# Conditional expert-weight loads in 1 MB pieces, and the weight conversion's DMAs issued at another point of the slot

## The chip, the cores and the metric

One Trainium2 chip, one of its cores. The metric is device time in microseconds (us) from launch to end, all in one program. A profiled execution also has a span, from its first to its last instruction.

## The reference

Three stages, each feeding the next, all in float32 results:

```python
# 1: attention, 8 x 8 heads, 576 tokens, head size 64, 32 memory slots
a = softmax(phi over tokens);  k_m = a^T k;  v_m = a^T v
x = softmax(q k_m^T / 8) v_m                    # -> [4608, 512]
# 2: top-1 mixture of 8 experts, 512 -> 1024 -> 512
e = argmax of the normalised x . expert_emb / tau;  g = its probability
x = g * (relu(x @ w1[e]) @ w2[e])
# 3: bilinear layer, 512 -> 1024 -> 1024 -> 512
out = ((x @ v1) * (x @ v2)) @ w3 @ w_out
```

The weights of stage 3 arrive as 64-bit floats. They have to be turned into 32-bit ones by integer operations on the chip.

## The kernel before

Matrix products are done to float32 accuracy by splitting each operand into a high and a low part and adding three products (`mm3`, lines 113 to 116, so a matmul shows there under line 114, 115 or 116).

Stage 2, the mixture, is the stage that is changed. The tokens are sorted by expert into slots of 128; a slot has one expert. `Moe.run` (line 1558) goes over 36 slots j; a few further slots are handled by `single` (line 1538) if they are used. Iteration j does the first product of slot j (`mm1`, output `hp`, 24 matmuls of 512 columns) and the second product of slot j-2 (`mm2`, output `py`, 24 matmuls). Between the two the hidden block must be transposed, and this goes through DRAM:

- `flip(j)` (line 1432): VectorE transposes 32 x 32 blocks of slot j+3's gathered tokens (line 1439) and of `hp` (line 1445) into the tile `T`, of which there is one, and SP (SyncE) issues the write of `T` to a DRAM scratch `scr` (line 1450, 768 KB). I call this the T write of iteration j.
- `unflip` (line 1453): four loads from `scr` into the tile `U`, of which there are two (line 1458, 4 x 192 KB). They are issued by SP when the T write has landed. I call these the U loads.
- `splith(j-1)` (line 1474), in iteration j: ScalarE makes the high part `hTh` (line 1481) from U of slot j-1, VectorE the low part `hTl` (line 1483). `splitx` makes the operands of a later `mm1` from the same U.

ScalarE, VectorE and SP each work through their instructions in program order. So VectorE does, in iteration j: `flip(j)`, a branch for an expert change in w1 (`split1`, line 1372), half of `splith(j-1)`, a branch for w2 (`split2`, line 1382), the other half, `splitx`, then `out2` of slot j-2 (line 1524), and the weight conversion described below.

Expert weights: w1 and w2 of an expert are 2 MB each, held raw in four tiles of 512 KB each (`r1`, `r2`, lines 1292 and 1293), and split into high and low parts (`share`, line 1355) when the next slot has another expert. Every iteration issues, on SP, eight conditional loads of 512 KB (`load1`, `load2`, lines 1335 to 1353): pieces 2 and 3 of w1 and of w2 behind the T write, pieces 0 and 1 of both behind the U loads. The condition is a register, read by SP once per slot (`regs`, lines 1330 and 1331). Where the expert does not change, a conditional load moves nothing, but SP still goes through its instructions. In this data four changes of expert lie in the loop.

The weight conversion for stage 3 is spread over the slots by `Moe2.early(s)` (line 1934), with s = j - 2, called at the end of iteration j (the argument `late`, line 1612; the argument `early`, line 1589, is empty). It has two DMA parts on SP: `load_raw` (line 1648, 512 KB of 64-bit weights into a tile `st`, shown in the trace as `st<-in_moe_w_dram`, 16 times, s from 0 to 22) and `keep` (line 1671, 512 KB of converted weights to DRAM, `wq<-w` at line 1672, 8 times, s from 4 to 25). Its compute part is `conv` (line 1656: one instruction on ScalarE, four on VectorE), two steps after the load. At steps s from 25 on, `early` also issues loads and transposes that prepare stage 3.

So SP's order in iteration j is: T write; w1 pieces 2, 3; w2 pieces 2, 3; four U loads; the register reads; w1 pieces 0, 1; w2 pieces 0, 1; a `keep` or a `load_raw` or both, in most iterations up to j = 27; then the T write of j+1.

Stage 3 follows (`Moe2.run`, line 1967): first 8 plain column groups, then four groups by a seven-product scheme for 2 x 2 blocks (`pair`, line 1860), whose matmuls are at line 1811.

Of the kernel before, what the change touches and what calls it, by code (L numbers as in the profile page):

```python
# [8 lines left out]
F32 = mybir.dt.float32  # L9
# [7 lines left out]
P = 128  # L17
B, H, S, D, M = 8, 8, 576, 64, 32
N = B * S
DM = H * D  # L20
E, F = 8, 1024
# [97 lines left out]
class Fillers:  # L119
    def __init__(self):  # L120
        self.q = []
# [4 lines left out]
    def run(self, n):  # L126
        while n > 0 and self.q:
            self.q.pop(0)()
            n -= 1
# [1158 lines left out]
class Moe:  # L1288
    def __init__(self, c, pool, w1, w2, xs, ys):
        self.c, self.pool = c, pool  # L1290
        self.w1, self.w2, self.xs, self.ys = w1, w2, xs, ys
        self.r1 = [pool.tile([P, F], F32, name=f"w1r{k}") for k in range(4)]
        self.r2 = [pool.tile([P, 2, DM], F32, name=f"w2r{k}") for k in range(4)]
        self.s1 = [
            (pool.tile([P, F], F32R, name=f"w1h{k}"), pool.tile([P, F], F32R, name=f"w1l{k}")) for k in range(4)
        ]
        self.xg, self.xT, self.h, self.hT = {}, {}, {}, {}
        self.sreg, self.py, self.u = {}, {}, {}
# [34 lines left out]
        return self.sreg[j]  # L1333

    def load1(self, j, ks=range(4)):
        e, f = self.regs(j)
        kw = {} if f is None else {"cond": f}
        for k in ks:
            self.c.nc.sync.dma_start(
                out=self.r1[k],  # L1340
                in_=self.w1[bass.ds(e, 1), k * P:(k + 1) * P, :].rearrange("a p f -> p (a f)"),
                **kw,
            )

    def load2(self, j, ks=range(4)):
        e, f = self.regs(j)
        kw = {} if f is None else {"cond": f}
        for k in ks:
            self.c.nc.sync.dma_start(
                out=self.r2[k],  # L1350
                in_=self.w2[bass.ds(e, 1), 2 * k * P:(2 * k + 2) * P, :].rearrange("a (u p) f -> p (a u) f", u=2),
                **kw,
            )

# [183 lines left out]
    def single(self, j):  # L1538
        c, nc = self.c, self.c.nc
        r = nc.values_load(c.nused[0:1, 0:1], min_val=0, max_val=NSLOT)  # L1540
        with c.tc.If(r > j):
# [13 lines left out]
            if j + 1 < NSLOT:  # L1555
                self.single(j + 1)

    def run(self, early, late):
        g = self.gates

        def groups(j, f, d):
            for a, b in ((j - j % GS, j - j % GS + GS), (NT, NT + 1)):
                if a == j - d or (a == NT and j == NT - 2 + d):
                    f(a, b)

        for j in range(NT):
            self.mm1(j)
            if j == 0:
                self.load1(0)
            if j < 2:  # L1570
                self.split1(j + 1)
            if j == 1:
                self.split2_first(2, 4)
            self.flip(j)
            if j < 2:
                self.load1(j + 1)
            else:
                if j > 2:
                    self.load1(j, (2, 3))
                self.load2(j - 2, (2, 3))  # L1580
                self.split1(j + 1)
            if j == 0:
                self.tx(2)
            if j + 4 <= NT:
                self.gather(j + 4)
            self.unflip()
            if j > 1:
                self.load1(j + 1, (0, 1))
            if j in early:
                early[j]()  # L1590
            if j == 1:
                self.load2(0, (0, 1))
            if j == 0:
                self.split2_first(0, 2)
            if j > 1:
                self.mm2(j - 2)
            if j > 0:
                self.splith(j - 1, (0,))
            if j > 1:
                self.split2(j - 1)  # L1600
                self.load2(j - 1, (0, 1))
            if j > 0:
                self.splith(j - 1, (1,))
            self.splitx(j + 2)
            if j == NEAR - 2:
                self.nexts()
            groups(j, g.norm, 0)
            groups(j, g.shift, 1)
            if j > 1:
                self.out2(j - 2)  # L1610
            groups(j, g.finish, 1)
            if j in late:
                late[j]()
        self.mm2(NT - 2)
        self.load2(NT - 2, (2, 3))
        self.splith(NT - 1, (0,))
        self.split2(NT - 1)
        self.load2(NT - 1)
        self.splith(NT - 1, (1,))
        self.out2(NT - 2)  # L1620
        self.mm2(NT - 1)
        self.out2(NT - 1)
        self.single(NT)


class Moe2:
# [304 lines left out]
            nc.scalar.copy(h, w[:, i])  # L1931
            nc.gpsimd.tensor_tensor(c.wpl[:, 2 * x + i, :], w[:, i], h.bitcast(F32), op=ALU.subtract)

    def early(self, s, pool):
        if s == 0:
            self.wpool = pool()
            self.mark = self.c.keep.tile([1, 1], F32, name="mark")
            self.wpt = {}
        for n in range(16):
            if s == self.at(n):  # L1940
                self.load_raw(n)
            if s == self.at(n) + 3 and n % 2:
                self.keep(n // 2)
        for n in range(16):
            if s == self.at(n) + 2:
                self.conv(n)
        if s in (25, 28):
            self.load_y(0, (s - 25) // 3)
        if s in (27, 29):
            self.flip_out(0, (s - 27) // 2)  # L1950
        if s in (28, 30):
            self.flip_in(0, (s - 28) // 2)
        if s in (29, 31):
            self.prep_plain((s - 29) // 2)
        if s in (27, 28):
            self.wload(s - 27)
        if s == 30:
            self.wsplit(0)
            self.wload(2)
        if s in (32, 33):  # L1960
            self.load_wp(s - 32)
# [95 lines left out]
@with_exitstack  # L2057
def kernel(
    ctx: ExitStack,
    tc: tile.TileContext,  # L2060
    q: bass.AP,
    k: bass.AP,
    v: bass.AP,
    phi: bass.AP,
    emb: bass.AP,
    tau: bass.AP,
    w1: bass.AP,
    w2: bass.AP,
    m2w1: bass.AP,
    m2w2: bass.AP,  # L2070
    m2w3: bass.AP,
    m2wout: bass.AP,
    const: bass.AP,
    out: bass.AP,
):
    nc = tc.nc
    c = Ctx()
    c.nc, c.tc = nc, tc
    c.keep = ctx.enter_context(tc.tile_pool(name="keep", bufs=1))
    dram = ctx.enter_context(tc.tile_pool(name="dram", bufs=1, space=bass.MemoryType.DRAM))  # L2080
    xs = dram.tile([N, XW], F32, name="xs")
    ys = dram.tile([N, YW], F32, name="ys")
    ctx.enter_context(tc.manual_schedule())
    c.wp = dram.tile([F, DM], F32, name="wp")
    c.wq = [dram.tile([P, 1024], F32, name=f"wq{i}") for i in range(8)]
    c.scr2 = [dram.tile([P, 4, 256], F32, name=f"scry{i}") for i in range(4)]
    c.scr = [dram.tile([P, 4, SH], F32, name=f"scr{i}") for i in range(4)]

    def pool(name, **kw):
        return tc.tile_pool(name=name, bufs=1, reuse_waits="tile", **kw)  # L2090

    def pspool(name):
        return pool(name, space=bass.MemoryType.PSUM)

    c.psw = ctx.enter_context(pspool("psw"))
    psa = ExitStack()
    c.ps = psa.enter_context(pspool("psa"))
    rst = ExitStack()
    c.rt = rst.enter_context(pool("rt", side="right"))
    with pool("attn", side="left") as p, pool("wprod", side="left") as pw:  # L2100
        setup_const(c, p, const, emb, tau)
        at = Attn(c, p, pw, q, k, v, phi, xs, m2w3, m2wout)
        at.run()
    mst = ExitStack()
    moe = Moe(c, mst.enter_context(pool("moe", side="left")), w1, w2, xs, ys)
    moe.second(mst.enter_context(pool("moeb", side="left")))
    rp = rst.enter_context(pool("rout", side="right"))

    moe.load1(-1)
    moe.load2(-1)  # L2110
    for j in range(3):
        moe.gather(j)
    moe.gates = Gates(c, mst.enter_context(pool("gates", side="left")))
    psa.close()
    psb = ExitStack()
    c.ps = psb.enter_context(pspool("psm"))
    moe.split1(0)
    moe.tx(0)
    at.wp.tail(moe.pool2)
    moe.tx(1)  # L2120
    moe.gates.rows(rp)
    rst.close()
    moe.gather(3)
    est = ExitStack()
    moe2 = Moe2(c, m2w1, m2w2, ys, out)
    mk = lambda: est.enter_context(pool("m2a", side="right"))

    steps = range(NT - 34, NT)
    moe.run({}, {j: (lambda s=j - steps[0]: moe2.early(s, mk)) for j in steps})
    mst.close()  # L2130
    with pool("moe2", side="left") as p:
        moe2.run(p)
    est.close()
    psb.close()
# [58 lines left out]
```

## Time and profile before

| what | value |
|---|---|
| median of 3 runs | 1320.77 us (1313.59 to 1321.11) |
| the profiled execution's own time | 1324.6 us |
| its span | 1322.8 us |
| TensorE busy, share of the span | 1208.6 us, 91% |
| VectorE, ScalarE, GpSimd busy | 877.7, 496.2, 569.8 us |
| mean granted TensorE clock | 0.968 |
| bytes moved by DMA | 228.66 MB |

How to read it: the profiled execution is one run, 3.8 us above the median of the unprofiled ones. The 1.8 us between its own time and its span lie outside the program's instructions. A busy TensorE is not TensorE at its peak, because matmuls overlap: a matmul row lasts about 0.4 us while a new one starts every 0.23 us. The mixture's loop runs from about 270 to 730 us of the span.

### The profile page before, as it was taken

The page shows a single profiled execution, that of the slowest core. Times are in us where ns is not written, and L with a number is a line of the kernel's source. Part 1 is how long each engine was busy: PE and PEld are TensorE (multiplying, and loading weights), DVE is VectorE, ACT ScalarE, POOL GpSimd, SP SyncE. Part 2 cuts the span into 40 slices and gives each one's busy share as a digit, 9 for nine tenths or more (in the row PEclk, how much of TensorE's full clock was granted, in tenths as well). Part 3 has the DMA queues.
Part 4 walks back from the last instruction along what each step waited for, and adds up shares of the span by engine and source line. Part 5 has one row for each costly group of instructions (what it writes and reads, how often), then busy time and mean ns, then how long its engine had stood idle before and what let it go on. Part 6 is the DMA issues. An engine that isn't in the chain of part 4 may idle for free. (4 is left out here: it accounts for less than half of the span.)

```text
span 1322.8 us, 19897 instructions
## 1 busy us (share of the span) xinstructions
PE 1208.6 (91%) x6124; PEld 948.9 (72%) x6124; DVE 877.7 (66%) x1706; ACT 496.2 (38%) x897; POOL 569.8 (43%) x705
## 2 busy tenths in 40 slices
PE   7788789899988998998899899999999999999996
PEld 6555566677767776776667677887878787788885
DVE  5898999876566667547666266728763874687262
ACT  4655455342233233123333154425433533435330
POOL 2685766622132232222232038715761674376222
PEclk9879889999999999999999899999999999999998
DMA  9999996567998778887876164415241532332001
GB/s 238 248 241 258 235 259 204 190 204 222 283 267 250 221 219 272 239 227 230 274 224 176 58 216 133 128 61 146 64 143 48 144 96 96 101 90 96 32 17 64
DMA packets 115215, 228.66 MB, mean 173 GB/s; under 512 B 11720, under 2 KB 73160, under 8 KB 115088
## 3 DMA queue, kind: packets, MB, share of 16 engines
q1 hardware_dynamic: 105824, 197.75, 52.5%
q0 software_dynamic: 8832, 28.92, 6.8%
q8 instruction: 50, 0.82, 0.3%
q14 instruction: 77, 0.63, 0.2%
q10 hardware_dynamic: 432, 0.55, 0.1%
HBM read 292.39 MB, written 72.40 MB: 276 GB/s over the span
## 5 line engine op out<-in xcount | busy, mean ns | idle before, releaser
L1483 DVE SCALAR_TENSOR_TENSOR hTl<-U,hTh 128x128 fp32r<-128x128 f32 x288 | 81.3, 344 | 117.7 <-ACT hTh L1481 89.9
L115 PE MATMUL hp<-w1l,xTh 128*128 128x512 f32 x296 | 122.1, 412 | 21.5 <-DVEq L1379 16.8
L114 PE MATMUL hp<-w1h,xTh 128*128 128x512 f32 x296 | 120.6, 408 | 14.1 <-ACT w1h L1359 10.9
L114 PE MATMUL py<-w2h,hTh 128*128 128x512 f32 x296 | 119.5, 404 | 10.9 <-ACTq L1385 10.9
L1529 POOL DMA_INDIRECT ys<-y,sidx x37 | 37.4, 1011 | 206.7 <-DVE y L1528 145.0
L1481 ACT ACTIVATE hTh<-U 128x512 fp32r<-128x512 f32 x72 | 45.3, 631 | 210.2 <-DMA U<-scr 108.1
L115 PE MATMUL py<-w2l,hTh 128*128 128x512 f32 x296 | 118.7, 401 | 1.3 <-DVE w2l L1360 0.8
L116 PE MATMUL py<-w2h,hTl 128*128 128x512 f32 x296 | 118.4, 400 | 1.4 <-DVE hTl L1483 1.4
L116 PE MATMUL hp<-w1h,xTl 128*128 128x512 f32 x296 | 119.2, 403 | 0.0
L1713 DVE TENSOR_TENSOR wgl<-sum,wgh 128x1024 fp32r<-128x1024 f32 x32 | 45.7, 1429 | 103.3 <-ACT wgh L1709 103.1
L116 PE MATMUL po<-wph,abl 128*128 128x512 f32 x288 | 112.8, 392 | 1.0 <-DVE abl L1858 0.7
L114 PE MATMUL po<-wph,abh 128*128 128x512 f32 x288 | 112.2, 390 | 0.0
L115 PE MATMUL po<-wpl,abh 128*128 128x512 f32 x288 | 112.1, 389 | 0.0
L1811 PE MATMUL pst<-xsh,wgh 128*128 128x512 f32 x256 | 101.2, 395 | 1.9 <-ACT pc L1879 1.5
L1713 POOL TENSOR_TENSOR wgl<-w,wgh 128x512 fp32r<-128x512 f32 x32 | 43.4, 1355 | 134.8 <-ACT wgh L1709 129.3
L1811 PE MATMUL pst<-xsl,wgh 128*128 128x512 f32 x256 | 100.3, 392 | 0.9 <-DVE xsl L1801 0.9
L1811 PE MATMUL pst<-xsh,wgl 128*128 128x512 f32 x256 | 100.0, 391 | 0.0
L115 PEld LDWEIGHTS hp<-w1l,xTh 128*128 128x128 f32 x296 | 57.5, 194 | 42.2 <-DVEq L1379 22.5
L114 PEld LDWEIGHTS hp<-w1h,xTh 128*128 128x128 f32 x296 | 57.3, 194 | 31.0 <-ACT w1h L1359 13.0
L114 PEld LDWEIGHTS py<-w2h,hTh 128*128 128x128 f32 x296 | 56.4, 191 | 27.8 <-ACTq L1385 13.5
L1857 ACT CAST abh<-pa 128x512 fp32r<-128x512 f32 x32 | 19.9, 622 | 148.5 <-DVE pa L1890 148.5
L115 PEld LDWEIGHTS py<-w2l,hTh 128*128 128x128 f32 x296 | 56.5, 191 | 16.1 <-DVEq L1385 1.7
(300 smaller groups left out, 3094.8 us busy)
## 6 DMA issues: line engine op xcount, KB each, us to landing
w2r<-in_moe_w_dram SPq DMA_DIRECT2D x152, 512.0 KB
w1r<-in_moe_w_dram SPq DMA_DIRECT2D x150, 512.0 KB
scr<-T SPq DMA_DIRECT2D x34, 768.0 KB
U<-scr SPq DMA_DIRECT2D x136, 192.0 KB
w<-wq SPq DMA_DIRECT2D x40, 512.0 KB
yin<-ys SPq DMA_DIRECT2D x36, 256.5 KB
qs<-in_q_dram SPq DMA_DIRECT2D x16, 576.0 KB
kv<-in_k_dram SPq DMA_DIRECT2D x32, 288.0 KB
```

The costliest lines, as they stand in the source:

```text
L114: nc.tensor.matmul(out, a[0], b[0], start=first, stop=False)
L115: nc.tensor.matmul(out, a[0], b[1], start=False, stop=False)
L116: nc.tensor.matmul(out, a[1], b[0], start=False, stop=last)
L1481: nc.scalar.activation(h4, u, ACTF.Relu)
L1483: nc.vector.scalar_tensor_tensor(l4[:, k], u[:, k], 0.0, h4[:, k].bitcast(F32), op0=ALU.max, op1=ALU.subtract)
L1529: nc.gpsimd.indirect_dma_start(out=self.ys, out_offset=bass.IndirectOffsetOnAxis(ap=c.sidx[:, j:j + 1], axis=0), in_=y, in_offset=None, bo ...
L1713: eng.tensor_tensor(l[:, s], src, h[:, s].bitcast(F32), op=ALU.subtract)
L1811: self.c.nc.tensor.matmul(out, ws[wi], x[xi], start=first and i == 0 and n == 0, stop=i == 1 and n == 2, skip_group_check=True,)
L1857: nc.scalar.copy(hi, pr)
```

## The change

The raw weights of an expert become two tiles of 1 MB for w1 and two for w2; the old names are views of their halves. A conditional load now fetches one 1 MB tile, so that an iteration issues four of them and not eight, at the same points. The DMA parts of the conversion (`load_raw`, `keep`) are split off from `early` into `before`, called in iteration j between the issue of the gather and `unflip`, that is behind the T write and its conditional loads, ahead of the U loads of the same iteration. The compute part stays where it was, at the end of the iteration, as do the preparations from s = 25 on.

```diff
-        self.r1 = [pool.tile([P, F], F32, name=f"w1r{k}") for k in range(4)]
-        self.r2 = [pool.tile([P, 2, DM], F32, name=f"w2r{k}") for k in range(4)]
+        self.d1 = [pool.tile([P, 2, F], F32, name=f"w1r{k}") for k in range(2)]
+        self.d2 = [pool.tile([P, 4, DM], F32, name=f"w2r{k}") for k in range(2)]
+        self.r1 = [self.d1[k // 2][:, k % 2, :] for k in range(4)]
+        self.r2 = [self.d2[k // 2][:, k % 2 * 2:k % 2 * 2 + 2, :] for k in range(4)]
...
     def load1(self, j, ks=range(4)):
+        self.load(j, ks, self.d1, self.w1, 2)
+
+    def load2(self, j, ks=range(4)):
+        self.load(j, ks, self.d2, self.w2, 4)
+
+    def load(self, j, ks, to, w, u):
         e, f = self.regs(j)
         kw = {} if f is None else {"cond": f}
-        for k in ks:
+        for k in sorted({k // 2 for k in ks}):
             self.c.nc.sync.dma_start(
-                out=self.r1[k],
-                in_=self.w1[bass.ds(e, 1), k * P:(k + 1) * P, :].rearrange("a p f -> p (a f)"),
+                out=to[k],
+                in_=w[bass.ds(e, 1), u * k * P:u * (k + 1) * P, :].rearrange("a (u p) f -> p (a u) f", u=u),
                 **kw,
             )
...
-    def run(self, early, late):
+    def run(self, before, early, late):
...
             if j + 4 <= NT:
                 self.gather(j + 4)
+            if j in before:
+                before[j]()
             self.unflip()
...
-    def early(self, s, pool):
+    def before(self, s, pool):
         if s == 0:
             self.wpool = pool()
...
             if s == self.at(n) + 3 and n % 2:
                 self.keep(n // 2)
+
+    def early(self, s):
         for n in range(16):
             if s == self.at(n) + 2:
                 self.conv(n)
```

## Rows read from the trace of the kernel before

**Rows 1.** Stretches: length; busy PE, weight loads, DVE, ACT, POOL; clock, DMA share, GB/s

```profile
279.00:754.00 475.00, 425.09 (x1734) 329.91 (x1732) 289.02 (x783) 131.62 (x237) 122.64 (x203) 0.97 0.78 228
754.00:1322.80 568.80, 553.09 (x2400) 448.90 (x2400) 347.20 (x441) 219.96 (x371) 280.74 (x305) 0.99 0.32 98
```

**Rows 2.** TensorE's waits: total us, times, longest

```profile
PE hp L115 <- DVEq L1379: 16.8, 13, 2.2
PE py L114 <- ACTq L1385: 10.9, 5, 3.7
PE hp L114 <- ACT w1h L1359: 10.9, 5, 4.1
```

**Rows 3.** Timeline of TensorE: start, us, what

```profile
454.01 0.39 PE L114 MATMUL py<-w2h,hTh 128*128 128x512 f32 x1
454.24 0.40 PE L115 MATMUL py<-w2l,hTh 128*128 128x512 f32 x1
```

**Rows 4.** Page, costliest groups: ScalarE's first step on U

```profile
L1481 ACT ACTIVATE hTh<-U 128x512 fp32r<-128x512 f32 x72 | 45.3, 631 | 210.2 <-DMA U<-scr 108.1
```

**Rows 5.** Timeline of SP, U loads of iteration 14 to T write of 15

```profile
453.43 1.75 SPq L1458 DMA_DIRECT2D U<-scr  x4
456.71 0.54 SPq L1339 DMA_DIRECT2D w1r<-in_moe_w_dram  x2
457.59 0.50 SPq L1349 DMA_DIRECT2D w2r<-in_moe_w_dram  x2
...
460.42 0.35 SPq L1450 DMA_DIRECT2D scr<-T  x1
```

**Rows 6.** Timeline of ScalarE, iteration 15: U of slot 14 arrives

```profile
459.67 0.63 ACT L1481 ACTIVATE hTh<-U 128x512 fp32r<-128x512 f32 x1 [4.70 <-DMA U<-scr]
```

**Rows 7.** Timelines of VectorE and SP around the T write of iteration 16

```profile
465.88 0.77 DVE L1439 STREAM_TRANSPOSE T<-xg 128x256 f32<-128x256 f32 x2 [1.74 <-DMA scr<-T]
466.62 1.30 DVE L1445 STREAM_TRANSPOSE T<-hp 128x512 f32<-128x512 f32 x2
...
470.60 0.35 SPq L1672 DMA_DIRECT2D wq<-w  x1
471.00 0.43 SPq L1651 DMA_DIRECT2D st<-in_moe_w_dram  x1
472.01 0.38 SPq L1450 DMA_DIRECT2D scr<-T  x1
...
480.47 1.77 SPq L1458 DMA_DIRECT2D U<-scr  x4
```

**Rows 8.** Timeline of SP, iteration 3, and the T write of iteration 34

```profile
299.57 0.53 SPq L1450 DMA_DIRECT2D scr<-T  x1
...
308.33 1.75 SPq L1458 DMA_DIRECT2D U<-scr  x4
...
711.30 0.60 SPq L1450 DMA_DIRECT2D scr<-T  x1
```

**Rows 9.** Timeline of SP, iteration 26

```profile
603.40 0.35 SPq L1450 DMA_DIRECT2D scr<-T  x1
...
606.75 1.91 SPq L1458 DMA_DIRECT2D U<-scr  x4
```

**Rows 10.** Timelines of SP and ScalarE, iteration 9, real w1 loads behind the T write

```profile
381.42 0.34 SPq L1450 DMA_DIRECT2D scr<-T  x1
382.06 1.58 SPq L1339 DMA_DIRECT2D w1r<-in_moe_w_dram  x2
...
385.96 1.80 SPq L1458 DMA_DIRECT2D U<-scr  x4
...
395.76 0.63 ACT L1481 ACTIVATE hTh<-U 128x512 fp32r<-128x512 f32 x1 [2.09 <-DMA U<-scr]
```

**Rows 11.** SP's own waits: total us, times, longest

```profile
SPq L1339 <- DMA w1r<-in_moe_w_dram: 6.5, 9, 3.6
SPq L1651 <- DMA U<-scr: 3.1, 5, 1.8
```

More of the change, by code (lines that the diff above doesn't have):

```diff
@@ L1335, in load1 @@
     def load1(self, j, ks=range(4)):
+        self.load(j, ks, self.d1, self.w1, 2)
+    def load2(self, j, ks=range(4)):
+        self.load(j, ks, self.d2, self.w2, 4)
+    def load(self, j, ks, to, w, u):
         e, f = self.regs(j)
         kw = {} if f is None else {"cond": f}
-        for k in ks:
+        for k in sorted({k // 2 for k in ks}):
             self.c.nc.sync.dma_start(
-                out=self.r1[k],
-                in_=self.w1[bass.ds(e, 1), k * P:(k + 1) * P, :].rearrange("a p f -> p (a f)"),
[L1342 to L1351, printed above, removed]
+                out=to[k],
+                in_=w[bass.ds(e, 1), u * k * P:u * (k + 1) * P, :].rearrange("a (u p) f -> p (a u) f", u=u),
                 **kw,
@@ L2128 @@
     steps = range(NT - 34, NT)
-    moe.run({}, {j: (lambda s=j - steps[0]: moe2.early(s, mk)) for j in steps})
+    moe.run(
+        {j: (lambda s=j - steps[0]: moe2.before(s, mk)) for j in steps},
+        {},
+        {j: (lambda s=j - steps[0]: moe2.early(s)) for j in steps},
+    )
     mst.close()
```

## The prediction

> **What bounds the kernel now.** The page first. It gives TensorE 91% of the span, so the question is where the other 9% lies. The busy time by stretches answers it: from 754 us to the end TensorE is busy 553.09 of 568.80 us, but in the mixture only 425.09 of 475.00 [rows 1]. The change touches the mixture alone, and the 50 us that TensorE lacks there are all there is to gain.
>
> Next the list of TensorE's waits. Its longest entries are at the mixture's lines [rows 2]: 16.8 us until VectorE is past the branch for w1, 10.9 us until ScalarE is past the branch for w2, and 10.9 us at an expert change, for the split weights. So TensorE waits for engines that reach a branch late, not for data of its own.
>
> What an iteration could take comes from the timeline of TensorE: a matmul starts every 0.23 us [rows 3], and an iteration has 48, so 48 x 0.23 = 11.0 us. What it takes: the T writes of iterations 3 and 34 start at 299.57 and 711.30 us [rows 8], that is (711.30 - 299.57) / 31 = 13.28 us each. The room is 2.2 us an iteration, 69 us over these 31, expert changes included.
>
> Why ScalarE and VectorE are late: ScalarE stood idle 210.2 us before its first instruction on U, 108.1 us of this directly put down to the U loads [rows 4]. Both engines work in order, so everything behind that instruction waits too: the halves of the split, the branches, and at last the next-but-one flip. This gives a loop over two iterations: T write of j, U loads of j, split of U in iteration j+1, flip and T write of j+2. What one iteration spends between its flip and the landing of its U is therefore paid once in two iterations, and half of it per iteration. I read the loop's SP part from the timelines, in three pieces.
>
> First, the T write is issued late. In iteration 16 the flip ended at 466.62 + 1.30 = 467.92, the write was issued at 472.01, 4.1 us later [rows 7]. I read this for all 36 iterations: in 18 of them (first 5, last 35) the write comes over 0.6 us late, 66.3 us in all; SP is still busy with what it issues between the U loads and the T write. Second, the write's own landing, from its issue to that of the U loads: 8.5 us in iteration 16, with a store and a load of 512 KB issued just ahead of it [rows 7], but 3.35 us in iteration 26, with nothing ahead [rows 9]. Over iterations 3 to 33 the mean is 7.16 us in the 15 that have a conversion DMA issued at most 4 us ahead (first: 8.76, [rows 8]) and 5.48 us in the other 16. Third, the U loads themselves, 6.2 us from 453.43 to ScalarE's start at 459.67 [rows 5, 6].
>
> **The change, part by part.** The sum is made against the profiled execution, 1324.6 us, of which 1.8 lie outside the span and stay.
>
> *A. SP's work between U loads and T write.* One pair of conditional loads takes 457.59 - 456.71 = 0.88 us of SP, so 0.44 each when nothing moves [rows 5]. Four go per iteration; the two behind the T write lie in the wait for its landing and are worth nothing (cover: at least the 3.35 us of iteration 26, [rows 9], against 1.8 us of work before and 0.9 after). The two behind the U loads are worth 0.88 us wherever the write is late. The store takes SP 471.00 - 470.60 = 0.40 us, the load 0.43 us [rows 7], and both leave this place. Of the 18 late writes, 8 have neither ahead of them (0.88 each, one only 0.83 as it is no later: 7.0 us), 3 a load (1.31 each: 3.9), 6 both (1.71 each: 10.3), 1 a store (1.28). Together 22.5 us of lateness go. Bounds: 0, if the flip or the other engines are late next, and 66.3 us, all the lateness.
>
> *B. The conversion's transfers no longer run ahead of the T write.* Fifteen writes land 7.16 - 5.48 = 1.7 us earlier: 25 us. But the transfers now lie between the T write and the U loads. What of them is hidden there? At full use the queues move 228 / 0.78 = 292 GB/s [rows 1], so the T write's 0.79 MB need 2.7 us, and of the 3.35 us of the quiet iteration [rows 9] 0.65 us is an empty queue; with about 0.4 us until the first U load is issued (1.75 us for four, [rows 5]) I estimate 1.0 us of cover. A load of 0.52 MB needs 1.8 us by the same rate. So 1.0 us in each of 15 iterations is a gain and the rest is given back in the U loads: 15 us. Bounds: 25 us, nothing given back, and a loss. For the loss the nearest row is iteration 9, where 1 MB of real weights follows the T write: U is there 395.76 - 385.96 = 9.8 us after its issue [rows 10], against 6.2 [rows 6], so 3.6 us more per MB. The 16 loads and 8 stores are 12.6 MB, so 45 us on the U loads, with 25 us back from the T writes: 20 us lost. I take the 15 us, because iteration 9's T write itself landed after 4.5 us [rows 10], in spite of the load behind it.
>
> Here the Trainium skill speaks against the change: "DMA: Bandwidth & Descriptors", section "Queues, rings and completion order", says that on each DMA engine the descriptors of one queue are taken up in the order of the ring. By that rule alone what leaves the front of the T write stands in front of the U loads, and B is worth nothing; that is the second rival below. Iteration 9's late U agrees with it, its early T write shows that the order is not all.
>
> *C. Pieces of 1 MB.* The bytes are the same. A 1 MB piece gives its first half only with its second, but the split comes long after: loads issued from 382.06 [rows 10] are split in the next change, about 100 us later. Cost 0; if that cover were gone, 0.5 MB / 292 GB/s = 1.8 us for each of the four changes and each of w1 and w2, 14 us.
>
> *D. Fewer DMAs in SP's order.* SP's own waits show issues held by the landing of earlier, unrelated transfers: 6.5 us for w1 loads at line 1339, 3.1 us for U loads at line 1651 [rows 11]. With nine to eleven DMAs an iteration in place of thirteen to fifteen such a hold should reach further back and be rarer. I take 0, bounds 0 and 9.6 us gained. The moved load and store wait for nothing new: their tiles were released by `conv` of an earlier iteration, which VectorE ends before the flip that the T write waits for.
>
> Sum: A and B shorten the path by 22.5 + 15 = 37.5 us, half of which counts, as the loop spans two iterations: 18.7 us, well inside the 69 us of room. 1324.6 - 18.7 = 1305.9 us for a profiled execution. That one was 3.8 us above the median of the runs, so I forecast 1320.8 - 18.7 = 1302 us for the median.
>
> **The rivals.** *All of it counts.* If the next T write, not the one after it, waits on this path (T is one tile, and VectorE's transposes wait for the write's landing, 1.74 us in [rows 7]), each us saved counts whole: 37.5 us, but no more than the two branch waits of rows 2, 16.8 + 10.9 = 27.7 us, can give, and a little of the changes' 10.9. I put 30 us: 1291 us. Against it: ScalarE's wait is for U, not for T [rows 4].
>
> *The order of the queue decides.* B is worth nothing, A half of 22.5 = 11.2 us: 1309.5 us. For it: iteration 9's U [rows 10].
>
> *The U loads become later than they were.* The moved transfers put 45 us on the U loads, and T writes that are issued and land earlier bring nothing. Place: ScalarE's instruction at line 1481. Half of 45 counts: 22.5 us, so 1343 us. Where the earlier T writes do count, A and B give 22.5 + 25 = 47.5 us, and it decides only from 47.5 / 12.6 = 3.8 us a moved MB. Iteration 9 shows 3.6, but with a full MB at once, where most of the iterations concerned move half of that; this speaks against it.
>
> *It doesn't do what it says:* skipped 1 MB loads cost SP as much as two of 512 KB. Then A has only the moved DMAs, 9 loads at 0.43 and 7 stores at 0.40, 6.7 us, and the time is 1320.8 - (6.7 + 15) / 2 = 1310 us. Nothing speaks for it.
>
> **How the numbers follow.** Forecast 0.42; all counts 0.2; queue order 0.23; U later 0.1; no saving on SP 0.05. A measurement of this kernel can tell about 1% from no change, 13.2 us, so "faster" is below 1307.6 us. The forecast, good to about 10 us, is below it with 0.7 (0.29); all counts 0.2; queue order, near the border, 0.08 (as D could help it). That is 0.57 for faster, 0.09 for slower (the rival above 1334, nearly whole), 0.34 for within 1%. The range goes from 1283 (beyond "all counts" by D's 9.6 us, less than full) to 1322 us: it leaves out the late U and little else.
>
> **What would show it.** Right: SP's line of conditional loads with 75 or so issues of each weight; the T write issued within 0.1 us of its flip's end in most iterations, and the sum of lateness down from 66 to about 44 us or less; T writes landing in 4 to 5.5 us also where a conversion is due; TensorE's waits at lines 114 and 115 for the two branches down by half; the mixture's stretch some 19 us shorter, the stage behind it as long as before. Wrong: ScalarE's idle time before line 1481 as large as before or larger, with U loads of 8 us and more in the iterations that move 1 MB, or lateness gone and TensorE's waits as long as before, which would say that another engine holds the loop.

## The result, and the profile after

The changed kernel takes 1306.28 us (median of 10 runs, 1303.86 to 1311.4) against 1320.83 us for the kernel before (10 runs): a ratio of 0.990, 95% interval 0.988 to 0.992. In a later comparison, among the experiments below, it came out at 0.986 (0.983 to 0.989). By these ratios it is 13 to 19 us faster, by the medians 14.5 and 17.6 us; a median of 1302 us was forecast.

The profiled execution took 1304.0 us, its span is 1302.2 us, 20.6 us less than before. The loop of the mixture, from the first T write to the 36th, went from 446.8 to 422.7 us, which is 24.1 us less. The rest is spread: the first T write comes 2.8 us later, and stage 3 takes 571.1 us where it took 568.9.

How much of a stretch is TensorE's is read first, as in [rows 1]. This is the view by stretches of the changed kernel (length; busy PE, weight loads, DVE, ACT, POOL; clock, DMA share, GB/s):

```profile
279.00:740.00 461.00, 433.25 (x1784) 342.44 (x1783) 293.76 (x791) 137.12 (x247) 127.56 (x208) 0.97 0.81 237
```

TensorE is busy 94% of it, against 89% [rows 1]. (The last 9 us of this stretch are stage 3 already, which starts at 731.1; without them it is 94% too.) TensorE's waits at the mixture's lines, in the changed kernel (total us, times, longest; lines 1357, 1377 and 1383 are lines 1359, 1379 and 1385 of before):

```profile
PE hp L115 <- DVEq L1377: 9.4, 6, 3.4
PE py L114 <- ACT w2h L1357: 7.4, 3, 2.8
...
PE py L114 <- ACTq L1383: 1.7, 1, 1.7
PE hp L114 <- ACT w1h L1357: 1.7, 1, 1.7
```

The wait for VectorE at the w1 branch fell from 16.8 to 9.4 us and that for ScalarE at the w2 branch from 10.9 to 1.7 [rows 2]. At an expert change the wait moved: w1's split is waited for 1.7 us, not 10.9, but w2's split, which was not among the long waits before, 7.4 us. All waits of `hp` and `py` together fell from 49 to 27 us. A second profile of the changed kernel, described below, has 13.4 us for VectorE at the w1 branch, 2.7 for w2's split and 36 in all, so single entries of this list differ by several us from one execution to the next.

The page's DMA issues show that the change does what it says. Its group for ScalarE's first step on U shows that ScalarE stands idle there about as long as it did, 204.7 us for 210.2, and that the part put down to the U loads grew from 108.1 to 114.8 us [rows 4]:

```profile
L1479 ACT ACTIVATE hTh<-U 128x512 fp32r<-128x512 f32 x72 | 45.3, 631 | 204.7 <-DMA U<-scr 114.8
...
w2r<-in_moe_w_dram SPq DMA_DIRECT2D x76, 1024.0 KB
w1r<-in_moe_w_dram SPq DMA_DIRECT2D x75, 1024.0 KB
```

Now the T write of iteration 16, the one of [rows 7]. VectorE's end of the flip in the changed kernel:

```profile
458.37 1.40 DVE L1443 STREAM_TRANSPOSE T<-hp 128x512 f32<-128x512 f32 x2 [1.10 <-PE hp L116]
```

and SP's timeline around it:

```profile
455.04 1.75 SPq L1456 DMA_DIRECT2D U<-scr  x4
458.34 0.09 SPq L1347 DMA_DIRECT2D w1r<-in_moe_w_dram  x1
458.78 0.09 SPq L1347 DMA_DIRECT2D w2r<-in_moe_w_dram  x1
459.80 0.35 SPq L1448 DMA_DIRECT2D scr<-T  x1
...
464.80 1.28 SPq L1456 DMA_DIRECT2D U<-scr  x3
```

The flip ends at 458.37 + 1.40 = 459.77 and the write is issued at 459.80, where it was 4.1 us late. SP was through with its conditional loads 0.9 us before. The write lands after 5.0 us, not 8.5. And the flip waited for TensorE (`hp`, 1.10 us), not for U or for the T write.

Iteration 9, the one of [rows 10], is of another kind. SP in the changed kernel:

```profile
375.39 0.36 SPq L1448 DMA_DIRECT2D scr<-T  x1
376.09 0.38 SPq L1347 DMA_DIRECT2D w1r<-in_moe_w_dram  x1
376.83 0.08 SPq L1347 DMA_DIRECT2D w2r<-in_moe_w_dram  x1
376.95 0.78 SPq L1672 DMA_DIRECT2D wq<-w  x1
377.78 0.46 SPq L1651 DMA_DIRECT2D st<-in_moe_w_dram  x1
378.86 2.18 SPq L1456 DMA_DIRECT2D U<-scr  x4
```

and ScalarE, when that U is there:

```profile
393.25 0.63 ACT L1479 ACTIVATE hTh<-U 128x512 fp32r<-128x512 f32 x1 [8.79 <-DMA U<-scr]
```

1 MB of new weights and 1 MB of conversion now stand between the T write and the U loads. The write still lands after 3.5 us, but U comes 393.25 - 378.86 = 14.4 us after its issue, 9.8 before. Iterations 9 and 10 take 31.8 us together where they took 28.6; 18 and 19, where the same meets, 31.4 for 26.2.

The three pieces of the path, read for all iterations as in the prediction:

```
                          before   after   after, second profile
T writes over 0.6 us late   18       9        9
  sum of lateness          66.3     24.8     23.5  us
T write, issue to U issue  6.29     5.52     5.80  us, mean of iterations 3 to 33
U loads to landing         6.80     7.44     7.63  us, mean of iterations 3 to 33
first to 36th T write     446.8    422.7    428.1  us
```

The second profile is of an execution of 1312.0 us, from the later comparison, the longest of its six there. Single executions differ by some us, so profiles are compared below in pairs where there are two.

### The profile page after: what moved, and what is told of

The parts are those of the page before. It is cut to its first block, busy times and chain, and to the rows that moved or that the text cites. A ratio compares the mean times of both kernels' runs of the same rounds, so it can differ in the third digit from the quotient of the medians.

```text
span 1302.2 us, 19324 instructions
## 1 busy us (share of the span) xinstructions
PE 1205.3 (93%) x6124; PEld 953.1 (73%) x6124; DVE 880.7 (68%) x1706; ACT 496.1 (38%) x897; POOL 568.3 (44%) x705
## 5 line engine op out<-in xcount | busy, mean ns | idle before, releaser
L1479 ACT ACTIVATE hTh<-U 128x512 fp32r<-128x512 f32 x72 | 45.3, 631 | 204.7 <-DMA U<-scr 114.8
L114 PEld LDWEIGHTS py<-w2h,hTh 128*128 128x128 f32 x296 | 57.4, 194 | 24.8 <-ACT w2h L1357 8.7
L115 PEld LDWEIGHTS py<-w2l,hTh 128*128 128x128 f32 x296 | 57.3, 194 | 17.5 <-DVE w2l L1358 3.2
```

The costliest lines, as they stand in the source:

```text
L114: nc.tensor.matmul(out, a[0], b[0], start=first, stop=False)
L115: nc.tensor.matmul(out, a[0], b[1], start=False, stop=False)
L1479: nc.scalar.activation(h4, u, ACTF.Relu)
```

## The experiments

All ratios are to the kernel before on the same chip, with 95% intervals. There were three comparisons, in which the kernel before took 1319.5, 1324.5 and 1324.7 us.

**Each half alone.** First only the merge: the changed kernel with the conversion's DMAs back at the end of the iteration.

```diff
     moe.run(
-        {j: (lambda s=j - steps[0]: moe2.before(s, mk)) for j in steps},
+        {},
         {},
-        {j: (lambda s=j - steps[0]: moe2.early(s)) for j in steps},
+        {j: (lambda s=j - steps[0]: (moe2.before(s, mk), moe2.early(s))) for j in steps},
     )
```

> Only the loads in 1 MB pieces; the conversion's DMAs stay at the end of the iteration. Theory A (SP's time between the U loads and the T write is what made the T writes late): 18 late writes x 0.88 us = 15.8 us, half of it, 7.9 us: ratio to before 0.994, lateness of the T writes down from 66 us to about 50. Rival (the merge gives nothing, the gain is all the moved DMAs): ratio 1.000 +- 0.002. Rival (halves add up to less than the whole, since either relieves the same wait): 0.992 or lower here and for the other half too.

Then only the move: the loads in eight pieces of 512 KB again.

```diff
-        self.d1 = [pool.tile([P, 2, F], F32, name=f"w1r{k}") for k in range(2)]
-        self.d2 = [pool.tile([P, 4, DM], F32, name=f"w2r{k}") for k in range(2)]
...
+        self.r1 = [pool.tile([P, F], F32, name=f"w1r{k}") for k in range(4)]
+        self.r2 = [pool.tile([P, 2, DM], F32, name=f"w2r{k}") for k in range(4)]
...
```

> Only the conversion's DMAs moved behind the T write; eight loads of 512 KB as before. Theory: A's other part 6.7 us and B's 15 us, half of 21.7: ratio to before 0.992, T writes landing within 5 us where a conversion is due. Rival (the transfers only change whom they delay): 3 us of SP time alone, 0.998. In iterations 9, 18 and 27, where 1 MB of new weights and the moved 1 MB meet, U should land 13 us after its issue here too, if the order on the queue and not the size of the pieces is the cause.

Measured: the merge 0.993 (0.990 to 0.996), the move 0.9905 (0.987 to 0.994). To see whether they add up, both ran again beside the whole change.

> The changed kernel once more, on the same chip and beside the same runs of the kernel before as the next three. Both theories: 0.990 +- 0.003.

> Only the merge, again, to be set beside the whole change on one chip. If the halves add up (each takes its own share of the T writes' way): this and the next together lose as much as the whole, so 0.994 here and 0.994 there with 0.988 to 0.990 for the whole. If either relieves the same wait: 0.993 here, 0.991 there, whole 0.990.

> Only the moved DMAs, again. As said of the run before: 0.994 if the halves add up, 0.991 if either relieves the same wait.

Measured: whole 0.986 (0.983 to 0.989), merge 0.993 (0.991 to 0.996), move 0.990 (0.987 to 0.993). The halves save 0.7 and 1.0%, 1.7% together, the whole 1.4%: within the intervals of this comparison they add up. Against the first result, 0.990 for the whole, they do not (0.993 x 0.990 = 0.983), so the whole may give less than its halves do apart; the profiles below say where. That the merge gives nothing is out.

The profiles show which piece each half takes. With the merge alone lateness falls to 42.5 and 44.6 us in two profiles, 22 to 24 less, and the T writes land as late as before (6.33 and 6.45 us). Iteration 16 of the merge alone, on SP:

```profile
465.97 0.35 SPq L1672 DMA_DIRECT2D wq<-w  x1
466.37 0.43 SPq L1651 DMA_DIRECT2D st<-in_moe_w_dram  x1
466.91 0.88 SPq L1448 DMA_DIRECT2D scr<-T  x1
...
475.56 1.77 SPq L1456 DMA_DIRECT2D U<-scr  x4
```

8.65 us, near the 8.46 us of [rows 7]: the store and the load still run ahead of the write. With the move alone the writes land after 4.83 and 5.10 us (4.79 and 5.19 in the 15 iterations that had a conversion DMA ahead of the write before, about the 5 us expected), but lateness is 52.8 and 53.1 us. Its iteration 16, VectorE, the end of the flip:

```profile
461.57 1.30 DVE L1445 STREAM_TRANSPOSE T<-hp 128x512 f32<-128x512 f32 x2
```

and SP, with two conditional loads of each weight, 0.88 us a pair:

```profile
462.22 0.54 SPq L1339 DMA_DIRECT2D w1r<-in_moe_w_dram  x2
463.10 0.50 SPq L1349 DMA_DIRECT2D w2r<-in_moe_w_dram  x2
463.96 0.35 SPq L1450 DMA_DIRECT2D scr<-T  x1
```

The flip ends at 462.87, the write comes 1.1 us later, behind the conditional loads. And U comes 13.3 and 14.4 us after its issue in iteration 9, as expected: the order of the issues does that, not the size of the pieces.

Lateness and landing are not independent. Iteration 19 of the move alone, VectorE's end of the flip and SP:

```profile
495.32 1.41 DVE L1445 STREAM_TRANSPOSE T<-hp 128x512 f32<-128x512 f32 x2 [0.38 <-PE hp L116]
504.76 0.35 SPq L1450 DMA_DIRECT2D scr<-T  x1
...
508.60 1.75 SPq L1458 DMA_DIRECT2D U<-scr  x4
```

The same iteration of the changed kernel, and last ScalarE, when U of iteration 18 is there:

```profile
491.95 1.40 DVE L1443 STREAM_TRANSPOSE T<-hp 128x512 f32<-128x512 f32 x2 [0.36 <-PE hp L116]
496.14 0.36 SPq L1448 DMA_DIRECT2D scr<-T  x1
...
506.25 1.74 SPq L1456 DMA_DIRECT2D U<-scr  x4
504.44 0.63 ACT L1479 ACTIVATE hTh<-U 128x512 fp32r<-128x512 f32 x1 [15.45 <-DMA U<-scr]
```

The write is 8.0 us late there and lands after 3.8; here it is 2.8 us late and lands after 10.1; it is issued 8.3 us before ScalarE has U of iteration 18. From the flip's end to the next U loads it is 11.9 us there and 12.9 here. Over the loop, the merge on top of the move takes 28 and 30 us from lateness and adds (5.52 - 4.83) x 31 = 21 and (5.80 - 5.10) x 31 = 22 us to the landings.

**SP's time, put back at two places.** To the changed kernel were added two register reads of about 0.6 us each on SP, from iteration 2 on.

```diff
             self.unflip()
+            if j > 1:
+                for _ in range(2):
+                    self.c.nc.sync.value_load(self.c.ej[0:1, j + 1:j + 2], min_val=0, max_val=E - 1)
```

> The changed kernel with two more register reads on SP behind each T write's conditional loads and the moved DMAs, ahead of the U loads, some 1.1 us of SP time that moves no byte and takes no DMA. Theory: this lies in the wait for the T write's landing, at least 3.3 us, and costs nothing: the ratio of the changed kernel, 0.990 +- 0.002. Rival (SP time counts wherever it lies, since SP works without a break): 36 x 1.1 = 40 us of SP, half of it on the path, 1.005.

This expectation is for reads ahead of the U loads. In the kernel that ran they stand behind `unflip`, behind the U loads, so the wait that it speaks of was not tested, and the run tests term A itself: 1.2 us of SP back in front of every T write. Measured: 0.996 (0.993 to 0.999). Lateness rose from 24.8 to 38.1 us, by 13.3. Half of that is 6.7 us, 0.5% of the time; the ratio is 0.6% above the 0.990 of the changed kernel, which did not run in this comparison. (The profiled execution, 1310.6 us, is 3 us below the median of this kernel, and its path as a whole is no longer than in the second profile of the changed kernel, so the medians carry this.) Next, the reads at the place that was meant:

```diff
             if j in before:
                 before[j]()
+            if j > 1:
+                for _ in range(2):
+                    self.c.nc.sync.value_load(self.c.ej[0:1, j + 1:j + 2], min_val=0, max_val=E - 1)
             self.unflip()
```

> The changed kernel with two more register reads on SP (about 1.2 us that moves no byte) between the moved DMAs and the U loads, so in the wait for the T write's landing; in the run before, the reads lay behind the U loads, ahead of the next T write, and the ratio was 0.996 where the changed kernel has 0.990. Theory (SP time counts only ahead of the T write): 0.990 +- 0.003, lateness of T writes about the 25 us of the changed kernel. Rival (SP time counts wherever it lies): 0.996, the U loads issued up to 1 us after the T write's landing.

Measured: 0.987 (0.984 to 0.990), 1307.1 us, lateness 23.8 us. The same reads cost nothing that can be told here, in the wait for the T write's landing. SP's time counts by its place.

**Where the conversion's DMAs stand.** Behind the U loads of the same iteration:

```diff
-            if j in before:
-                before[j]()
             self.unflip()
+            if j in before:
+                before[j]()
```

> The changed kernel, but the conversion's DMAs issued behind the U loads of the same iteration, ahead of the register reads, instead of ahead of the U loads. Theory (in the changed kernel the moved transfers cost the U loads about 0.6 us on average, 4 to 7 us in iterations 9 and 18, and a T write has slack against them now that SP is early): 0.985 to 0.988 to before, so 2 to 6 us below the changed kernel; U landing in 6 us in most iterations and under 11 in 9 and 18. Rival (what counts is that nothing stands ahead of the T write): 0.993 or more, T writes landing late again where a conversion is due, 7 us.

Measured: 0.990 (0.9865 to 0.994), the same as the changed kernel: a miss for the theory's number, and the rival's, 0.993 or more, lies at the edge of the interval. Both were half right. U lands after 6.86 us on average and after 10.9 and 7.7 in iterations 9 and 18, as the theory said, and the two pairs take 29.4 and 25.9 us. But T writes land after 6.6 us where a conversion was due before, near the rival's 7, and lateness is back at 47.1 us, as SP has the two issues ahead of the next T write again. The one pays for the other.

On ScalarE's queue, at the place of the changed kernel in the program:

```diff
-        self.c.nc.sync.dma_start(
+        self.c.nc.scalar.dma_start(
             out=raw.rearrange("p (a n) t -> p a (n t)", a=4),
...
-        self.c.nc.sync.dma_start(out=self.c.wq[f], in_=self.wide.rearrange("p u n -> p (u n)"))
+        self.c.nc.scalar.dma_start(out=self.c.wq[f], in_=self.wide.rearrange("p u n -> p (u n)"))
```

> The changed kernel with the conversion's load and store issued by ScalarE at the same point of the program, so on another DMA queue and not on SP. If it is their place in SP's queue, ahead of the U loads, that makes U late: U lands in 6 to 7 us on average (7.4 in the changed kernel), ratio 0.985 or lower. If it is the bytes, whatever the queue: U as late as in the changed kernel, 7.4 us, T writes later instead, ratio 0.990 +- 0.003.

Measured: 0.988 (0.985 to 0.991), 1308.6 us. Iteration 9 of this kernel, SP:

```profile
380.61 0.35 SPq L1448 DMA_DIRECT2D scr<-T  x1
...
386.86 1.93 SPq L1456 DMA_DIRECT2D U<-scr  x4
```

and ScalarE:

```profile
379.53 0.35 ACTq L1672 DMA_DIRECT2D wq<-w  x1
379.92 0.45 ACTq L1651 DMA_DIRECT2D st<-in_moe_w_dram  x1
...
394.92 0.63 ACT L1479 ACTIVATE hTh<-U 128x512 fp32r<-128x512 f32 x1 [2.10 <-DMA w1r<-in_moe_w_dram]
```

U is there 8.1 us after its issue, not 14.4; but now the T write takes 6.25 us, not 3.5. From T write to U it is 14.3 us here and 17.9 in the changed kernel. Over all iterations U gained 0.4 us and the T writes lost 0.4 (5.96 us) against the first profile of the changed kernel, 0.6 and 0.2 against the second, and the time is that of the changed kernel. ScalarE reaches the place in the program at another time than SP: here it issues the two 1.1 and 0.7 us ahead of the T write, in other iterations up to 7 us ahead or 4 us behind. So this run changes the queue and the time of issue together, and which of the two shifts the delay from U to the T write is not shown; on average it made no difference to the time.

**The conversion two iterations later**, so that it does not meet the new w1 weights:

```diff
-        return n * 3 // 2
+        return n * 3 // 2 + 2
```

> The changed kernel with the whole conversion two iterations later, so that no load or store of it falls into iterations 9, 18 and 27, where new w1 weights follow the T write. Theory (what the change gives back, it gives back where 1 MB of weights and 1 MB of conversion stand together ahead of the U loads): U lands there in about 10 us, not 14, the pairs of iterations 9 and 10, 18 and 19 take 29 and 26 us, not 32 and 31.5, and the ratio is 0.985. Rival (the late U of these iterations is made by the weights alone): U 13 us there, ratio 0.990.

Measured: 0.994 (0.990 to 0.997), 1315.4 us: a miss. The pairs behaved as expected, 28.4 and 26.7 us, with U after 9.1 and 8.0 us. But new w2 weights follow the T writes of iterations 11 and 20, and there the conversion now meets them. Iteration 11 of this kernel, SP:

```profile
407.77 0.35 SPq L1448 DMA_DIRECT2D scr<-T  x1
...
408.91 0.38 SPq L1347 DMA_DIRECT2D w2r<-in_moe_w_dram  x1
409.34 0.96 SPq L1672 DMA_DIRECT2D wq<-w  x1
410.34 0.58 SPq L1651 DMA_DIRECT2D st<-in_moe_w_dram  x1
413.00 2.54 SPq L1456 DMA_DIRECT2D U<-scr  x4
```

U lands 13.6 us after its issue there and 12.7 in iteration 20; these two and their successors take 27.9 and 27.0 us, where the changed kernel takes 22.0 and 21.3. The meeting moved, it did not end. The profile puts these two pairs 5.9 and 5.7 us behind the changed kernel's; the gain at the other two, 3.4 and 4.7 us, is smaller.

**Stage 3's preparation moved too.** The loads of y, of its transposed blocks and of weights in iterations 27 to 35 are issued in `before`:

```diff
+        if s in (25, 28):
+            self.load_y(0, (s - 25) // 3)
+        if s in (28, 30):
+            self.flip_in(0, (s - 28) // 2)
+        if s in (27, 28):
+            self.wload(s - 27)
+        if s in (32, 33):
+            self.load_wp(s - 32)
...
     def early(self, s):
```

> The changed kernel with the DMAs that prepare stage 3 in iterations 27 to 35 (loads of y, of its transposed blocks and of converted weights) moved behind the T write too. Theory: of the 24.8 us of lateness left, iterations 28, 31 and 33 hold 14.2, and half of that counts: 7 us, ratio 0.984 to 0.986. Rival (these iterations wait for something else): 0.990 +- 0.003.

Measured: 0.986 (0.982 to 0.989), 1305.4 us. The ratio is as the theory has it, but in this comparison the changed kernel itself did not run; by medians the two are 1 to 2 us apart, which can't be told from no difference. And lateness fell only from 24.8 to 20.7 us, not by 14.2, as iteration 28 stayed late (8.0 us, 6.7 in the changed kernel). So the mechanism that it names is mostly a miss.

**Bytes taken away.** One of the 16 loads of 64-bit weights is made and 15 are left out, 7.9 MB:

```diff
-        raw = self.raw[n] = self.st().bitcast(I32).rearrange("p (n t) -> p n t", t=2)
+        if n:
+            self.raw[n] = self.raw0
+            return
+        raw = self.raw0 = self.raw[n] = self.st().bitcast(I32).rearrange("p (n t) -> p n t", t=2)
```

> The changed kernel with one of the 16 loads of 64-bit weights made and the other 15 left out; every conversion reads the tile of the first one, so the weights of stage 3 are not the given ones. 7.9 MB fewer to move in the loop. Theory (what is left of TensorE's waits comes from U landing late behind the bytes of the queue): U lands in 6.5 us on average, TensorE waits 8 us less, 0.980 to 0.984. Rival (the loop is at what TensorE and the expert changes allow): as the changed kernel, 0.990 +- 0.003.

Measured: 0.981 (0.978 to 0.983), 1300.4 us, beside 0.986 and 1307.1 us for the changed kernel on the same chip. The same stretch in this kernel, and then in the second profile of the changed kernel:

```profile
279.00:740.00 461.00, 433.20 (x1799) 342.12 (x1798) 296.82 (x793) 138.38 (x248) 129.50 (x209) 0.97 0.76 221
```

```profile
279.00:740.00 461.00, 423.80 (x1749) 331.11 (x1748) 290.46 (x788) 132.87 (x240) 126.61 (x207) 0.98 0.81 235
```

The DMA share falls from 0.81 to 0.76, TensorE does 1799 matmuls in it and not 1749, and its waits at `hp` and `py` fall from 36 to 27 us. But the first profile of the changed kernel has 27 us of these waits too, with all the loads, so that fall isn't clear of the difference between executions. U lands after 7.04 us, not 7.63 (7.44 in the first profile); a fall to 6.5 us was expected. What carries the result are the medians: the bytes in the loop, with their issues, are a part of what is left, 7 us for 7.9 MB, which at the 292 GB/s of the prediction are 27 us of transfer.

No kernel here beats the changed one by more than its interval, apart from the last, which leaves work out.

## Why the prediction was right

The mechanism was right: a loop over two iterations, whose SP part the change shortens. That the time came out near the forecast is in part luck, as two terms were wrong in opposite directions and a third was left out.

**The loop over two iterations: right, and it is what the runs bear out best.** By it, what the three pieces of the path lose counts half. Worked out for each profile (lateness, plus 31 times the means of T write and U) and halved, against the loop's own change:

```
kernel                        half of the path's change   loop's change, us
whole change, two profiles       -22.7   -16.1             -24.1   -18.7
merge alone, two profiles        -13.9    -8.5             -12.1   -10.1
move alone, second profile       -13.4                     -16.0
behind the U loads               -16.8                     -18.1
SP reads behind U, ahead of U    -16.8   -18.6             -15.8   -20.4
ScalarE's queue                  -21.0                     -21.4
stage 3's preparation moved      -19.7                     -18.1
two iterations later             -16.9                     -12.8
15 loads left out                -35.3                     -26.8
```

Within some 4 us all agree except the last. Both columns come from one trace: they must agree as long as the rest of the loop, from the landing of U to the flip after the next, takes as long as before, so the table tests this. In the last row that rest grew by 17 us; why is not shown (an iteration takes 12.4 us there, where TensorE alone would need 11.0). In the first profile of the move alone, landings could not all be told apart, so it is left out.

**A, lateness: the right mechanism, its price too low, and not all of it a gain.** The sum put 22.5 us; the two profiles of the changed kernel show 66.3 - 24.8 = 41.5 and 42.8. The merge alone removes 22 to 24 and the move alone 13, where the working gave 15.8 and 6.7. The reads put back behind the U loads, 13.3 us of lateness, and ahead of them, none, show that it is SP's time at this place. Of what the working missed, one part is D, below: with the merge alone holds ahead of late writes fell by 5 us. With the move alone D went the other way, and some 15 us more lateness went than the two issues and D account for. There the T writes land 1.2 to 1.5 us earlier, so the U loads are issued earlier, and so is all of SP's work behind them; that this is the cause fits, but no run tests it alone. And lateness that goes can come back as landing, as in iteration 19 above, so the 41.5 us are not all won.

**B, the moved transfers: sized too high.** T writes land (6.29 - 5.52) x 31 = 24 us earlier in the first profile, as forecast (25), and 15 in the second. Given back on U were to be 10 us; it is (7.44 - 6.80) x 31 = 20 us, and 26 in the second. So B's net is 4 us, or a loss of 11, not 15 us gained. With the move alone it is (6.29 - 5.10) x 31 - (7.55 - 6.80) x 31 = 14 us in the second profile, as forecast, though both parts were larger, so the estimate of 1.0 us of cover held on balance only without the merge. The T writes show it too: 4 to 5.5 us were to be seen also where a conversion had been due, and in these 15 iterations it is 4.79 and 5.19 us with the move alone, but 6.24 and 6.50 in the changed kernel. Iteration 9's T write in [rows 10], on which the choice between the bounds rested, did show that a write is not held up by a load behind it. But a write that goes ahead of a load issued later agrees with the order of the queue; it does not speak against it, as the prediction has it, and it said nothing of U. For the whole change the second rival was nearer on B. The Trainium skill says in "DMA: Bandwidth & Descriptors", section "Queues, rings and completion order", that on each DMA engine the descriptors of one queue are taken up in ring order. The trace agrees with it: U comes 14.4 us after its issue behind 2 MB on its own queue in iteration 9, 8.1 us with half of these on another. As these were also issued 1.1 us before the T write there, this does not prove the rule. What A and B were wrong by has opposite signs, 41.5 + 4 = 45.5 us in the first profile and 42.8 - 11 = 32 in the second against 37.5, and so the total came out near.

**C: right on its own count.** The merge alone costs nothing at a change: TensorE's wait for w1's split is 10.4 and 10.9 us with it, 10.9 before. The move exchanges this wait for another. With the move alone it is 0.9 and 2.3 us, and TensorE waits 4.8 and 6.9 us for w2's split, behind the late U of iterations such as 9 and 18; in the two profiles of the changed kernel 1.7 and 2.1 us for w1's, 7.4 and 2.7 for w2's. With the conversion behind the U loads w1's wait is 8.8 us and w2's does not appear. The prediction has nothing of this exchange.

**D: not nothing, as taken.** SP's hold behind w1 loads fell from 6.5 to 1.5 us and behind U at line 1651 from 3.1 to 1.2 [rows 11], but a new one of 9.2 us, behind the conversion's load at the conditional loads, came in:

```profile
SPq L1347 <- DMA st<-in_moe_w_dram: 9.2, 3, 4.2
...
SPq L1347 <- DMA w1r<-in_moe_w_dram: 1.5, 1, 1.5
...
SPq L1651 <- DMA U<-scr: 1.2, 4, 0.5
```

The totals look even, but the place counts: the new hold lies behind the T write, ahead of the U loads. Read one by one, SP's holds by the landing of a DMA between the U loads and the next T write are 16.4 us before, 9.5 of them ahead of late writes. With the merge alone they are 7.4 and 9.0 us (4.5 and 4.0), with the move alone 23.2 and 21.4 (18.0 and 17.5), in the changed kernel 7.7 and 10.4 (2.9 and 2.6). So fewer DMAs did make such holds rarer where they count, by 6 to 9 us, near the bound of 9.6 that the prediction named and did not take.

**The rivals.** *All of it counts* needed 30 us; the loop gained 18.7 to 24.1 and the kernel 13 to 19, where the path became 45.5 and 32 us shorter. *U becomes later than it was* is true of U by 0.6 us on average and by 4.6 us in iteration 9, but not of the time, since T writes that come early do count. One sign of being wrong that the prediction named is half there: ScalarE's idle time before its first step on U hardly fell, and U comes after 14.4 and 13.7 us in iterations 9 and 18, though after 6.6 to 8.1 in the other five iterations that move a load and a store. *It doesn't do what it says* is out: lateness, and the ratio of the merge alone.

**The size.** 18.7 us were forecast. In the first comparison (1 - 0.9899) x 1320.8 = 13.3 us were measured, with an interval of 11 to 16, in the last (1 - 0.9859) x 1324.7 = 18.7 us, with one of 15 to 22. By the first the forecast is somewhat too large, by the last it is met; which is nearer can't be told from these runs.

## What to carry to other kernels

In a loop through DRAM, measure each piece (issue, landing, first use) for every iteration and find over how many iterations the loop goes; a saving counts by that share, and that held here, within 4 us, in every variant but one. Here the issuing engine's time was free in the wait for a landing and cost where a dependent transfer came next, so move work into such a wait, but count the bytes: what left the front of one transfer stood in front of the next. Another queue or another iteration changed only whom they delayed. And a transfer issued earlier is not a gain before it also lands earlier: read the two together.

## What was not expected of the hardware

A conditional load that moves nothing takes SP 0.44 us, whether it would fetch 512 KB or 1 MB: 0.88 us a pair before [rows 5], and 458.78 - 458.34 = 0.44 us from one to the next in the changed kernel. That was assumed. Not expected was that in iteration 9, with 2 MB ahead of them on the queue, the U loads land after 14 us while the T write issued just before these bytes lands after 3.5 us, near the 3.35 us of a write with no transfer of the conversion and no new weights around it [rows 9].
